# Strassen products of an expert kernel: common sums kept in PSUM, products of neighbouring steps interleaved, PReLU as a signed maximum, token sums of the attention on GpSimd

## The chip, the cores and the metric

The kernel runs on one core of one Trainium2 chip. The metric is the device time of one execution in microseconds (us). The engines are named as in the profile: PE is TensorE (matmul), PEld its weight loads, DVE VectorE, ACT ScalarE, POOL GpSimd, and SP SyncE, whose queue issues all DMAs here. Each of PE, DVE, ACT, POOL and SP works through its own instructions in the order in which the program gives them, and waits at the first one whose semaphores are not there yet.

## The reference

Three layers follow each other. Only what matters is shown.

```python
# 1. decayed linear attention, B=2, H=8, S=768, D=64 (tokens: B*S = 1536, width H*D = 512)
state = gamma * state + k_t v_t^T ;  y_t = scale * q_t . state
x = y.transpose(0, 2, 1, 3).reshape(1536, 512)
# 2. eight dense experts, F = 1024, gate made doubly stochastic in 8 rounds
P = exp(x @ w_gate - max); 8 times: P /= P.sum(1) + 1e-9; P /= P.sum(0) + 1e-9; P *= N / E
out = sum over e of P[:, e:e+1] * (np.maximum(x @ w1[e], 0) @ w2[e])
# 3. one layer of width 2048 with a learned slope per hidden unit
h = out @ w_in
y = (np.maximum(h, 0) + alpha * np.minimum(h, 0)) @ w_out
```

## The kernel before

The kernel has an attention stage and then 20 phases. A phase is one half of the tokens (768) through one block of 1024 hidden units: phases 0 to 15 are the two halves through the eight experts, phases 16 to 19 the two halves through the two halves of layer 3 (called the PReLU phases here, since their hidden units are max(h, 0) + alpha min(h, 0)). All products are fp32 split into a high and a low part, three matmuls for each (`mm3`).

A phase has two parts. In the first (L1 here), x times w1 is made by a Strassen-Winograd scheme for each of four column blocks j (n counts these steps over all phases): seven products of 6 matmuls each, `product(ph, j, p)`, in the order p = 1, 5, 6, 7, 4, 2, 3. Product 1 opens a PSUM bank, and product 2 is added into it; product 5 opens one, and product 3 is added into it; 6, 7 and 4 each have their own. `after` makes the four output blocks out of them: ACT copies product 1 to SBUF (`pu`, L475), DVE adds product 6 to it (L477), product 7 to that (L480), and three more additions (L481, L484, L489) make the blocks. `block` then applies Relu or PReLU and leaves a high part `hh` and a low part `hl`. The low part is put off by one product (`late`). In a PReLU phase a block is ACT Relu of -h (L458), ACT times -alpha (L459), DVE max and add (L460), ACT high part (L461), DVE low part (L462). In the second part (L2 here), `layer2` multiplies the blocks by w2, six tiles t0 to t5 of 48 matmuls of 512 columns.

The order of everything else is a table of hooks (`at`), each run behind one product or one tile: the splits of the next weights (`w1_adds`, `w1_part`, `w2_split`, with an ACT copy for the high part and POOL or DVE for the low part), the gate's rounds (`shift`, `cols`), decoding of the float64 weights of layer 3 (`decode`), the transposed copies of the experts' output for layer 3 (`turn`, in phases 8 and 16), and the sums of x that the scheme needs (`x_sums`, seven pieces for each of two k).

The attention stage runs 12 steps of 128 tokens: `prep(i+1)` (k scaled on POOL, L235), `scores` (PE, then DVE times the mask into A, L224), `state` (PE, then DVE scales the state into T, L261), `outs` (PE, then DVE, L297), `gate`. The dictionary `early` puts the weight splits and the x sums of phase 0 (L139 to L149, on DVE) behind steps 2 to 11.

## Time and profile before

| what | value |
|---|---|
| median of 3 runs | 1444.62 us (1437.99 to 1685.13) |
| profiled execution, time | 1439.99 us |
| its span, first to last instruction | 1438.2 us |
| mean granted TensorE clock | 0.969 |
| PE / DVE / ACT / POOL busy | 94% / 58% / 38% / 36% of the span |

The profiled execution has 1.8 us around its span and lies 4.6 us under the median of the three runs. Busy time of PE is counted from pipelined matmuls, so 94% doesn't say that PE has no time to give; the stages have to be looked at apart.

### The profile page before, as it was taken

Reading aid. Unit: us, or ns where it says so; the run is one execution under the profiler, and the core shown is the slowest. Engines: PE = TensorE matmul, PEld = TensorE weight load, DVE = VectorE, ACT = ScalarE, POOL = GpSimd, SP = SyncE. Lnnn points to the kernel's source line nnn. Section 1 sums busy time; section 2 is a strip of 40 time slices with the busy share of each in tenths; the row PEclk is TensorE's granted clock in tenths of the full one; section 3 lists DMA queues with packets and bytes.
Section 4 is the critical chain, followed back from the end, with each engine's and each line's share of the span. In section 5 each row is a group of like instructions: output and inputs, shape, how many; then the busy total and the mean of one; then the engine's idle time right before and its main releaser. Section 6 shows DMA issues by size and latency. Waiting matters only on the chain.

```text
span 1438.2 us, 18384 instructions
## 1 busy us (share of the span) xinstructions
PE 1356.9 (94%) x7045; PEld 1208.8 (84%) x7046; DVE 833.6 (58%) x1526; ACT 543.5 (38%) x979; POOL 520.7 (36%) x393
## 2 busy tenths in 40 slices
PE   9789999999999999999999999999998797887978
PEld 7688989889898988989898898989897677676876
DVE  4856565766666665766666666645457424564351
ACT  0242514243241423534242433414235626455360
POOL 3551515245251524426151543615243305042140
PEclk9899999999999999999999999999999898998989
DMA  8531223343342334244333333213032312221001
GB/s 300 179 104 53 87 84 107 97 119 92 110 125 81 110 96 124 83 124 118 101 110 96 103 98 108 84 56 89 30 125 63 101 35 74 80 81 59 30 30 44
DMA packets 45448, 136.25 MB, mean 95 GB/s; under 512 B 5169, under 2 KB 10289, under 8 KB 45361
## 3 DMA queue, kind: packets, MB, share of 16 engines
q1 hardware_dynamic: 45360, 135.08, 30.3%
q8 instruction: 55, 0.90, 0.2%
...
## 4 chain that ended last, share of the span: by engine, by line
PE 68%; issue 10%; ACT 7%; DVE 7%; POOL 6%; DMA 2%; SPq 0%; POOLq 0%; DVEq 0%; ACTq 0%
PE o L124 15%; PE o L122 15%; PE o L123 15%; PE p L124 7%; PE p L122 7%; PE p L123 7%; ACT n L459 3%; DVE p L460 2%; ACT n L458 2%; ACT hh L461 1%; DMA xd<-tt 1%; DMA kv<-in_kv_dram 1%; DVE p L481 1%; DVE u L480 1%; PE sc L216 1%
## 5 line engine op out<-in xcount | busy, mean ns | idle before, releaser
L92 POOL TENSOR_TENSOR s<-raw 128x256 f32<-128x256 f32 x42 | 37.5, 892 | 506.3 <-DVE wc69l L83 31.8
L451 ACT ACTIVATE hh<-p 128x384 fp32r<-128x384 f32 x256 | 120.4, 490 | 162.7 <-DVE p L481 135.1
L452 DVE SCALAR_TENSOR_TENSOR hl<-p,hh 128x384 fp32r<-128x384 f32 x256 | 136.5, 554 | 58.2 <-ACT hh L451 48.7
L520 DVE SCALAR_TENSOR_TENSOR acc<-o,P,acc 128x512 f32<-128x512 f32 x84 | 62.9, 749 | 153.2 <-PE o L124 153.2
L477 DVE TENSOR_TENSOR pu<-p,pu 128x384 f32<-128x384 f32 x80 | 44.5, 556 | 94.1 <-PE p L124 86.0
L411 ACT ACTIVATE ex<-ex,ebias 128x512 uint32<-128x512 uint32 x32 | 23.2, 725 | 193.3 <-DVE ex L410 188.5
L460 DVE SCALAR_TENSOR_TENSOR p<-p,n 128x384 f32<-128x384 f32 x64 | 36.3, 567 | 91.4 <-ACT n L459 91.4
L475 ACT ACTIVATE pu<-p 128x384 f32<-128x384 f32 x80 | 39.2, 490 | 65.1 <-PE p L124 65.0
L480 DVE TENSOR_TENSOR u<-p,pu 128x384 f32<-128x384 f32 x80 | 44.6, 557 | 21.5 <-PE p L124 17.5
L489 DVE TENSOR_TENSOR p<-p,pu 128x384 f32<-128x384 f32 x80 | 44.9, 562 | 14.4 <-PE p L124 13.8
L481 DVE TENSOR_TENSOR p<-p,u 128x384 f32<-128x384 f32 x80 | 45.3, 567 | 2.8
L461 ACT ACTIVATE hh<-p 128x384 fp32r<-128x384 f32 x64 | 31.5, 492 | 40.5 <-DVE p L460 40.5
L484 DVE TENSOR_TENSOR p<-p,u 128x384 f32<-128x384 f32 x80 | 44.5, 556 | 0.0
L458 ACT ACTIVATE n<-p 128x384 f32<-128x384 f32 x64 | 31.3, 490 | 31.3 <-DVE p L481 22.4
L410 DVE TENSOR_SCALAR ex<-rd 128x512 uint32<-128x512 uint32 x32 | 19.5, 609 | 39.5 <-DMA rd<-in_w_out_dram 19.9
L459 ACT ACTIVATE n<-n,nal 128x384 f32<-128x384 f32 x64 | 39.4, 616 | 2.1
L514 ACT ACTIVATE acc<-o 128x512 f32<-128x512 f32 x18 | 10.8, 598 | 75.3 <-PE o L124 75.3
L95 POOL TENSOR_TENSOR raw<-raw,s 128x256 f32<-128x256 f32 x42 | 35.4, 843 | 3.3
L462 DVE TENSOR_TENSOR hl<-p,hh 128x384 fp32r<-128x384 f32 x64 | 35.2, 550 | 1.6
L94 POOL TENSOR_TENSOR s<-raw 128x256 f32<-128x256 f32 x42 | 34.2, 814 | 0.0
L93 POOL TENSOR_TENSOR s<-s,raw 128x256 f32<-128x256 f32 x42 | 31.8, 758 | 3.3
L148 ACT ACTIVATE xh<-ta 128x384 fp32r<-128x384 f32 x16 | 8.4, 526 | 62.2 <-DVE ta L139 60.4
...
## 6 DMA issues: line engine op xcount, KB each, us to landing
raw<-in_w_dram SPq DMA_DIRECT2D x128, 512.0 KB, 3.7
raw<-wd SPq DMA_DIRECT2D x32, 512.0 KB, 3.3
rd<-in_w_in_dram SPq DMA_DIRECT2D x16, 512.0 KB, 4.2
...
rd<-in_w_out_dram SPq DMA_DIRECT2D x16, 512.0 KB, 4.2
qk<-in_qkT_dram SPq DMA_DIRECT2D x12, 512.0 KB, 5.1
kv<-in_kv_dram SPq DMA_DIRECT2D x12, 512.0 KB, 5.6
...
```

The costliest lines, as they stand in the source:

```text
L122: nc.tensor.matmul(ps, ah, bh, start=first, stop=False, skip_group_check=True)
L123: nc.tensor.matmul(ps, ah, bl, start=False, stop=False, skip_group_check=True)
L124: nc.tensor.matmul(ps, alo, bh, start=False, stop=last, skip_group_check=True)
L451: nc.scalar.activation(out=hi, in_=src, func=AF.Relu)
L452: late.append(lambda: nc.vector.scalar_tensor_tensor(out=lo, in0=src, scalar=0.0, in1=hi.bitcast(F32), op0=ALU.max, op1=ALU.subtract))
L458: nc.scalar.activation(out=neg, in_=src, func=AF.Relu, scale=-1.0)
L459: nc.scalar.activation(out=neg, in_=neg, func=AF.Copy, scale=nal[:, f:f + 1])
L460: nc.vector.scalar_tensor_tensor(out=src, in0=src, scalar=0.0, in1=neg, op0=ALU.max, op1=ALU.add)
L461: nc.scalar.activation(out=hi, in_=src, func=AF.Copy)
L480: nc.vector.tensor_tensor(out=u, in0=ps, in1=pu[n][:, 1], op=add)
L481: nc.vector.tensor_tensor(out=ps, in0=banks[n, 5], in1=u, op=add)
L520: nc.vector.scalar_tensor_tensor(out=acc[t], in0=ps, scalar=p, in1=acc[t], op0=ALU.mult, op1=ALU.add)
```

## The change

What it does, part by part:

- The sums that several blocks share are kept in PSUM. ACT copies product 1 from its bank A into a second bank B, and product 6 is added into B by PE. Product 5 is copied to SBUF (`d`, by ACT in expert phases, by DVE in PReLU phases). DVE writes B + d into a bank E, into which product 3 is added; product 7 is added into B; DVE writes B + d over bank D as the (1,1) block; product 4 is added into B as the (1,0) block. Four banks are written once by a matmul of ones before their first use (`seeded`).
- The products of step j stand between those of step j-1: (j,1), (j,5), (j-1,4), (j,6), (j-1,3), (j,2), (j,7).
- PReLU is max(s h, s alpha h) times s with s = -1 where alpha > 1 and 1 elsewhere: ACT makes s alpha h, and one product later DVE the maximum and ACT the high part, and one later DVE the low part.
- The x sums of phase 0 go to POOL in pieces, behind steps 6 to 11; the splits of step 0's weights come earlier, those of step 1's weights go to DVE behind the attention; k is scaled on ACT from step 7 on (eight instructions for each). s and s alpha are made on DVE at the start.
- Hooks of the weight splits move; `turn` uses plain fp32 matmuls with the identity in place of transposes; the gate's column sums go to other columns of a bank that DVE clears first.

```diff
@@ start of the attention stage
-            nc.scalar.activation(out=nal, in_=al, func=AF.Copy, scale=-1.0)
+            nc.vector.tensor_scalar(out=sg, in0=al, scalar1=1.0, scalar2=-2.0, op0=ALU.is_gt, op1=ALU.mult)
+            nc.vector.tensor_scalar_add(sg, sg, 1.0)
+            nc.vector.tensor_tensor(out=sa, in0=sg, in1=al, op=ALU.mult)
@@ prep
+                    if i <= NCH:
...
+                    else:
+                        for h in range(H):
+                            nc.scalar.activation(
+                                out=k_t[i][:, h, :], in_=kv_t[i][:, 0, h, :], func=AF.Copy, scale=Gk[:, c, h:h + 1]
+                            )
@@ early
+            xs = [x_pieces(0, k, xf[:, k, :], xf[:, 2 + k, :], pool) for k in range(2)]
             early = {
...
+                1: [lambda: w_load(0, 0)],
+                2: [lambda: w1_adds(0, pool)],
+                3: [lambda: w1_part(0, "a", pool), lambda: w_load(0, 1)],
+                4: [lambda: w1_part(0, "c", pool), lambda: w_load(1, 0)],
+                5: [lambda: w1_part(0, "b", pool), lambda: w_load(1, 1)],
+                6: xs[0][0:2],
+                7: xs[0][2:5],
+                8: xs[0][5:7],
+                9: xs[1][0:2],
+                10: xs[1][2:5],
+                11: xs[1][5:7],
@@ behind the attention
             nc.vector.tensor_copy(P, gt)
+            w1_adds(1, nc.vector)
+            for part in "acb":
+                w1_part(1, part, nc.vector)
@@ product
+        def seeded(name):
+            ps = bank(name)
+            if made[0] < 4:
+                made[0] += 1
+                nc.tensor.matmul(ps, one[:, 0:128], one, start=True, stop=True)
+            return ps[:, 0:HT]
...
-            key = {2: 1, 3: 5}.get(p, p)
+            key = {1: "A", 2: "A", 5: "D", 6: "B", 7: "B", 4: "B", 3: "E"}[p]
@@ block, PReLU
-            nc.scalar.activation(out=neg, in_=src, func=AF.Relu, scale=-1.0)
-            nc.scalar.activation(out=neg, in_=neg, func=AF.Copy, scale=nal[:, f:f + 1])
-            nc.vector.scalar_tensor_tensor(out=src, in0=src, scalar=0.0, in1=neg, op0=ALU.max, op1=ALU.add)
-            nc.scalar.activation(out=hi, in_=src, func=AF.Copy)
-            late.append(lambda: nc.vector.tensor_tensor(out=lo, in0=src, in1=hi.bitcast(F32), op=ALU.subtract))
+            nc.scalar.activation(out=t, in_=src, func=AF.Copy, scale=sa[:, f:f + 1])
+            def largest():
+                nc.vector.scalar_tensor_tensor(out=src, in0=src, scalar=s1, in1=t, op0=ALU.mult, op1=ALU.max)
+                nc.scalar.activation(out=hi, in_=src, func=AF.Copy, scale=s1)
+            late.append([largest, lambda: nc.vector.scalar_tensor_tensor(
+                out=lo, in0=src, scalar=s1, in1=hi.bitcast(F32), op0=ALU.mult, op1=ALU.subtract
+            )])
@@ after
+            if p == 5:
+                d = banks[n, "d"] = tmp.tile([128, HT], F32, tag="d", bufs=2, name=f"d{n}")
+                if PHASES[ph][1] < E:
+                    nc.scalar.activation(out=d, in_=banks[n, "D"], func=AF.Copy)
+                else:
+                    nc.vector.tensor_copy(d, banks[n, "D"])
+            elif p == 1:
+                banks[n, "B"] = seeded(f"B{n}")
+                nc.scalar.activation(out=banks[n, "B"], in_=banks[n, "A"], func=AF.Copy)
             elif p == 6:
-                nc.vector.tensor_tensor(out=pu[n][:, 1], in0=ps, in1=pu[n][:, 0], op=add)
+                banks[n, "E"] = seeded(f"E{n}")
+                nc.vector.tensor_tensor(out=banks[n, "E"], in0=banks[n, "B"], in1=banks[n, "d"], op=add)
             elif p == 7:
...
+                nc.vector.tensor_tensor(out=banks[n, "D"], in0=banks[n, "B"], in1=banks[n, "d"], op=add)
@@ turn
-                nc.tensor.transpose(ps[:, 128 * q:128 * q + 128], acc[3 * h + q][:, 128 * a:128 * a + 128], ident)
+                nc.tensor.matmul(
+                    ps[:, 128 * q:128 * q + 128], acc[3 * h + q][:, 128 * a:128 * a + 128], ident,
...
@@ hooks and order
-                at(ph, (j, 4), lambda m=m: w1_part(m, "c", pool))
-                at(ph, (j, 3), lambda m=m: w1_part(m, "a", pool))
-                at(ph, (j + 1, 5), lambda m=m: w1_part(m, "b", pool))
-            for j, key in enumerate(((0, 2), (1, 2), (2, 6), (3, 6))):
+                at(ph, (j, 2), lambda m=m: w1_part(m, "a", pool))
+                at(ph, (j, 7), lambda m=m: w1_part(m, "c", pool))
+                at(ph, (j, 3), lambda m=m: w1_part(m, "b", pool))
+            for j, key in enumerate(((2, 1), (2, 2), (3, 1), (2, 3))):
...
-        order = [(j, p) for j in range(NJ) for p in (1, 5, 6, 7, 4, 2, 3)] + [f"t{t}" for t in range(TT)]
+        order = [(0, 1), (0, 5), (0, 6), (0, 2), (0, 7)]
+        for j in range(1, NJ):
+            order += [(j, 1), (j, 5), (j - 1, 4), (j, 6), (j - 1, 3), (j, 2), (j, 7)]
+        order += [(NJ - 1, 3), (NJ - 1, 4)] + [f"t{t}" for t in range(TT)]
```

How the instructions stand, at three places. First ACT in one round (one j) of a PReLU phase, phase 17, before: `pu` is product 1, `n` the scaled block, `hh` the high part of a block, and `w` and `v` are splits of weights.

```order
L475 ACTIVATE pu_10908<-p_1_10901 128x384
L82 ACTIVATE wb70h<-raw_70_10667 128x512
L458 ACTIVATE n_11_10949<-p_7_10937 128x384
L459 ACTIVATE n_11_10949<-n_11_10949,nal 128x384
L461 ACTIVATE hh_11_10947<-p_7_10937 128x384
L458 ACTIVATE n_10_10964<-p_4_10954 128x384
L459 ACTIVATE n_10_10964<-n_10_10964,nal 128x384
L461 ACTIVATE hh_10_10962<-p_4_10954 128x384
L82 ACTIVATE wc71h<-s_10911 128x768
```

The same engine in a round of the same phase now; A, B, D and E are the PSUM banks.

```order
L532 ACTIVATE B_10719<-A_10712 128x384
L502 ACTIVATE hh_11_10701<-D_10631,sg 128x384
L83 ACTIVATE v68h<-raw_68_10233 128x1024
L498 ACTIVATE n_10_10748<-B_10621,sa 128x384
L502 ACTIVATE hh_10_10746<-B_10621,sg 128x384
L498 ACTIVATE n_01_10768<-E_10657,sa 128x384
L83 ACTIVATE wb71h<-raw_71_10496 128x512
L498 ACTIVATE n_00_10785<-A_10712,sa 128x384
L502 ACTIVATE hh_01_10766<-E_10657,sg 128x384
L83 ACTIVATE v69h<-raw_69_10287 128x1024
L498 ACTIVATE n_11_10804<-D_10730,sa 128x384
L502 ACTIVATE hh_00_10783<-A_10712,sg 128x384
```

A block has two ACT instructions in place of three, and between them stands the first one of the next block; in this round two `v` splits stand between them as well.

Second, DVE at the start of the program, before (A is the masked scores of step 0, `al` the slopes):

```order
L208 MEMSET ones 128x128
L224 TENSOR_TENSOR A_178<-sc_0_179,mask 128x4x128
L224 TENSOR_TENSOR A_178<-sc_1_180,mask 128x4x128
L261 TENSOR_TENSOR T_122<-st_196,tab 64x4x64 x2
L224 TENSOR_TENSOR A_216<-sc_0_217,mask 128x4x128
```

And now:

```order
L218 TENSOR_SCALAR sg<-al 128x16
L219 TENSOR_SCALAR sg<-sg 128x16
L220 TENSOR_TENSOR sa<-sg,al 128x16
L225 MEMSET ones 128x128
L241 TENSOR_TENSOR A_185<-sc_0_186,mask 128x4x128
L241 TENSOR_TENSOR A_185<-sc_1_187,mask 128x4x128
```

Three instructions on the slopes stand ahead of the first masked scores; the DMA of the slopes keeps its place on SP.

Third, DVE behind step 6 of the attention, before (`xc` is the step's output, `xl` the low parts of the x pieces, T the scaled state):

```order
L297 TENSOR_TENSOR xc_518<-y_509,tab 128x512
L139 TENSOR_TENSOR ta_0_529<-xf 128x384
L140 TENSOR_TENSOR ta_0_529<-xf,ta_0_529 128x384
L141 TENSOR_TENSOR tb_0_530<-xf 128x384
L142 TENSOR_TENSOR tb_0_530<-xf,ta_0_529 128x384
L149 TENSOR_TENSOR xl_0_163<-xf,xh_0_162 128x384
...
L149 TENSOR_TENSOR xl_0_167<-xf,xh_0_166 128x384
L261 TENSOR_TENSOR T_121<-st_483,tab 64x4x64 x2
L224 TENSOR_TENSOR A_561<-sc_0_562,mask 128x4x128
```

And now:

```order
L321 TENSOR_TENSOR xc_542<-y_533,tab 128x512
L285 TENSOR_TENSOR T_122<-st_500,tab 64x4x64 x2
L241 TENSOR_TENSOR A_577<-sc_0_578,mask 128x4x128
L241 TENSOR_TENSOR A_577<-sc_1_579,mask 128x4x128
L321 TENSOR_TENSOR xc_603<-y_590,tab 128x512
```

The eleven instructions of the x sums are gone from between `xc` and T.

## Rows read from the trace of the kernel before

**Rows 1.** The page: busy us, share of the span and instructions of each engine.

```profile
PE 1356.9 (94%) x7045; PEld 1208.8 (84%) x7046; DVE 833.6 (58%) x1526; ACT 543.5 (38%) x979; POOL 520.7 (36%) x393
```

**Rows 2.** Busy time by stretch; columns in the first line, PEclk is the granted clock.

```profile
core 0: us, PE busy (x) PEld busy (x) DVE busy (x) ACT busy (x) POOL busy (x), PEclk, DMA share, GB/s
0.00:76.10 76.10, 64.76 (x739) 54.16 (x740) 48.75 (x81) 11.88 (x22) 31.48 (x37) 0.91 0.67 231
76.10:114.60 38.50, 34.13 (x175) 33.21 (x176) 25.41 (x58) 16.01 (x30) 20.97 (x14) 0.91 0.33 101
148.70:1093.60 944.90, 938.35 (x4707) 844.40 (x4706) 587.56 (x1043) 345.32 (x615) 370.79 (x270) 1.00 0.33 98
1031.40:1061.10 29.70, 29.52 (x170) 29.20 (x169) 18.28 (x34) 15.97 (x29) 20.97 (x14) 1.00 0.28 91
1061.10:1093.60 32.50, 32.50 (x145) 26.88 (x144) 22.08 (x41) 10.74 (x21) 3.76 (x4) 1.00 0.30 95
1093.60:1434.50 340.90, 285.51 (x1273) 249.06 (x1272) 152.54 (x290) 163.30 (x301) 94.23 (x68) 0.90 0.18 58
1184.10:1229.40 45.30, 35.48 (x170) 34.04 (x169) 22.22 (x43) 29.23 (x53) 20.94 (x14) 0.85 0.18 59
45.90:52.70 6.80, 3.35 (x33) 3.04 (x34) 6.16 (x10) 0.00 (x0) 3.48 (x3) 0.50 0.05 16
```

**Rows 3.** Timeline of phase 17: one PReLU block on ACT and DVE, idle in brackets.

```profile
1203.03 0.49 ACT L458 ACTIVATE n<-p 128x384 f32<-128x384 f32 x1 [1.37 <-DVE p L481]
1203.55 0.61 ACT L459 ACTIVATE n<-n,nal 128x384 f32<-128x384 f32 x1
1204.20 0.57 DVE L460 SCALAR_TENSOR_TENSOR p<-p,n 128x384 f32<-128x384 f32 x1 [1.21 <-ACT n L459]
1204.80 0.49 ACT L461 ACTIVATE hh<-p 128x384 fp32r<-128x384 f32 x1 [0.63 <-DVE p L460]
1205.27 0.50 ACT L458 ACTIVATE n<-p 128x384 f32<-128x384 f32 x1
```

**Rows 4.** The page's DMA issues: the weights' loads, KB, median us to landing.

```profile
raw<-in_w_dram SPq DMA_DIRECT2D x128, 512.0 KB, 3.7
```

**Rows 5.** Timeline of the attention stage: start, duration, instruction, idle before it.

```profile
8.61 1.29 DVE L224 TENSOR_TENSOR A<-sc,mask 128x512 f32<-128x512 f32 x2 [7.62 <-DMA mask<-in_cmask_dram]
...
11.58 1.09 PE L284 MATMUL y<-A,kv 128*64 128x128 f32 x16
...
14.27 1.16 PE L274 MATMUL y<-qk,T 128*128 128x128 f32 x8
...
14.61 0.21 ACT L203 ACTIVATE nal<-al 128x16 f32<-128x16 f32 x1 [12.59 <-DMA al<-in_alpha_dram]
...
17.37 0.69 PE L250 MATMUL st<-kv,k 128*64 128x64 f32 x16
...
22.18 0.69 PE L250 MATMUL st<-kv,k 128*64 128x64 f32 x16
...
44.79 3.69 DVE L149 TENSOR_TENSOR xl<-xf,xh 128x384 fp32r<-128x384 f32 x2
...
49.35 1.12 PE L250 MATMUL st<-kv,k 128*64 128x64 f32 x16 [4.77 <-issue]
...
64.60 1.12 PE L250 MATMUL st<-kv,k 128*64 128x64 f32 x16 [4.06 <-issue]
```

**Rows 6.** Timeline of phase 8: three transposes and the matmul behind them.

```profile
596.01 0.49 PE L535 MATMUL tr<-ident,acc 128*128 128x128 f32 x3
596.25 0.42 PE L122 MATMUL p<-xh,wb32h 128*128 128x384 f32 x1
```

**Rows 7.** Groups of the attention stage: count, busy us, mean ns of one, idle.

```profile
L83 POOL TENSOR_TENSOR wa0l<-raw,wa0h 128x512 fp32r<-128x512 f32 x1 | 1.3, 1273 | 0.0
L82 ACT ACTIVATE wc1h<-s 128x768 fp32r<-128x768 f32 x1 | 0.8, 843 | 3.0 <-POOL s L94 3.0
```

**Rows 8.** Timeline of the attention stage: two ACT copies behind each other.

```profile
42.98 0.92 ACT L148 ACTIVATE xh<-xf 128x384 fp32r<-128x384 f32 x2
```

More of the change, by code (lines that the diff above doesn't have):

```diff
@@ L359, in shift @@
         def shift():
-            ps = bank("mx")
-            nc.tensor.matmul(ps[:, 0:128], ones, sums["m"], start=True, stop=True)
+            ps = bank("mx")[:, HT:512]
+            nc.vector.memset(ps, 0.0)
+            nc.tensor.matmul(ps, ones, sums["m"], start=False, stop=True, skip_group_check=True)
             nm = sp.tile([128, 1], F32, tag="nm", name="nm")
-            nc.vector.tensor_reduce(out=nm, in_=ps[:, 0:128], axis=AX.X, op=ALU.max)
+            nc.vector.tensor_reduce(out=nm, in_=ps, axis=AX.X, op=ALU.max)
             nc.vector.tensor_scalar_mul(nm, nm, -1.0)
@@ L380, in cols @@
         def cols(it):
-            ps = bank(f"cs{it}")
-            nc.tensor.matmul(ps[:, 0:E], ones, sums[it], start=True, stop=True)
+            ps = bank(f"cs{it}")[:, HT:HT + E]
+            nc.vector.memset(ps, 0.0)
+            nc.tensor.matmul(ps, ones, sums[it], start=False, stop=True, skip_group_check=True)
             g = sp.tile([128, E], F32, tag="g", name=f"g{it}")
-            nc.vector.tensor_scalar_add(g, ps[:, 0:E], 1e-9)
+            nc.vector.tensor_scalar_add(g, ps, 1e-9)
             nc.vector.reciprocal(out=g, in_=g)
@@ L426, in decode @@
                 decode_load(then)
-        banks, pu, hq, late = {}, {}, {}, []
+        banks, hq, late = {}, {}, []
+        made = [0]
+        def seeded(name):
[4 more added lines that the diff above has]
+            return ps[:, 0:HT]
         def product(ph, j, p):
             n = NJ * ph + j
-            key = {2: 1, 3: 5}.get(p, p)
-            if key == p:
-                banks[n, p] = bank(f"p{n}_{p}")[:, 0:HT]
+            key = {1: "A", 2: "A", 5: "D", 6: "B", 7: "B", 4: "B", 3: "E"}[p]
+            if p in (1, 5):
+                banks[n, key] = bank(f"{key}{n}")[:, 0:HT]
             ps = banks[n, key]
@@ L441, in product @@
                 ks = slice(128 * k, 128 * k + 128)
-                mm3(ps, wh[:, ks], wl[:, ks], xh[:, k, :], xl[:, k, :], k == 0 and key == p, k == 1)
+                mm3(ps, wh[:, ks], wl[:, ks], xh[:, k, :], xl[:, k, :], k == 0 and p in (1, 5), k == 1)
             after(ph, n, j, p)
@@ new lines, in largest, with step_late @@
+            def largest():
[3 more added lines that the diff above has]
+                out=lo, in0=src, scalar=s1, in1=hi.bitcast(F32), op0=ALU.mult, op1=ALU.subtract
+            )])
+        def step_late(steps):
+            for fns in steps:
+                fns.pop(0)()
+                if fns:
+                    late.append(fns)
@@ L464, in flush @@
         def flush():
             while late:
-                late.pop(0)()
+                steps = list(late)
+                late.clear()
+                step_late(steps)
         def after(ph, n, j, p):
             add = ALU.add
-            ps = banks[n, {2: 1, 3: 5}.get(p, p)]
             before = list(late)
             late.clear()
-            if p == 1:
-                pu[n] = tmp.tile([128, 2, HT], F32, tag="pu", bufs=2, name=f"pu{n}")
-                nc.scalar.activation(out=pu[n][:, 0], in_=ps, func=AF.Copy)
+            if p == 5:
[7 more added lines that the diff above has]
+                nc.scalar.activation(out=banks[n, "B"], in_=banks[n, "A"], func=AF.Copy)
@@ L482, in after @@
-                block(ph, n, j, 1, 1, ps)
+                nc.vector.tensor_tensor(out=banks[n, "D"], in0=banks[n, "B"], in1=banks[n, "d"], op=add)
+                block(ph, n, j, 1, 1, banks[n, "D"])
             elif p == 4:
-                nc.vector.tensor_tensor(out=ps, in0=ps, in1=pu[n, 3], op=add)
-                block(ph, n, j, 1, 0, ps)
+                block(ph, n, j, 1, 0, banks[n, "B"])
             elif p == 2:
-                block(ph, n, j, 0, 0, ps)
+                block(ph, n, j, 0, 0, banks[n, "A"])
@@ L488, in after @@
             elif p == 3:
-                nc.vector.tensor_tensor(out=ps, in0=ps, in1=pu[n][:, 1], op=add)
-                block(ph, n, j, 0, 1, ps)
-            for fn in before:
-                fn()
+                block(ph, n, j, 0, 1, banks[n, "E"])
+            step_late(before)
         acc, ob = {}, {}
@@ L534, in turn @@
             for q in range(3):
-                nc.tensor.transpose(ps[:, 128 * q:128 * q + 128], acc[3 * h + q][:, 128 * a:128 * a + 128], ident)
+                nc.tensor.matmul(
+                    ps[:, 128 * q:128 * q + 128], acc[3 * h + q][:, 128 * a:128 * a + 128], ident,
+                    start=(q == 0), stop=(q == 2), skip_group_check=True,
+                )
             t = tp.tile([128, HT], F32, tag="tmp", name=f"tt{g}_{a}{h}")
```

68 lines of the change are left out of this document (33 added, 35 removed).

## The prediction, made before the changed kernel ran

> **What bounds the kernel now.** I read the page first: PE is busy for 94% of the span, every other engine for 58% or less [rows 1]. That is a mean over stages, so next comes busy time by stretch. Phase 15 (1031.4 to 1093.6) shows what a phase costs when nothing holds PE: L1 29.7 us, nearly all of it PE, with the weight loads busy for 29.2 of them, and L2 32.5 us, at full clock [rows 2]. 168 matmuls in 29.7 us are 0.177 us each, 1.06 us a product. No part of the change takes matmuls away, so 62.2 us a phase is the floor that I measure the rest against. Phases 1 to 15 take 944.9 us [rows 2]; 15 floors are 933.0, and the 24 transposes of phase 8 add 8 x 0.24 = 1.9 (three of them push the next matmul back by 0.24 us [rows 6]). So at most 10 us lie there, although DVE is busy for 587.6 us of that stretch [rows 2].
>
> The four PReLU phases are another matter: 340.9 us against 4 x 62.2 + 1.9 = 250.7, so 90.2 us are lost, with the clock at 0.90 of full speed [rows 2]. In L1 of phase 17 (45.3 us) PE is busy for 35.5, ACT for 29.2, DVE for 22.2: nobody is full. The timeline says why. ACT starts a block at 1203.03, waits 0.63 us inside it for DVE's result, and starts the next block at 1205.27 [rows 3]: 2.24 us of ACT's queue per block, four blocks, 9 us for a round whose seven products need 7.4; the copy of product 1 and the weight splits come on top. The queue of ACT with its wait inside each block is the bound there, and PE stops, and its clock falls to half, behind it.
>
> The attention stage with phase 0's L1 takes 76.1 + 38.5 us [rows 2]. A step lasts 4.81 us (17.37 to 22.18) and PE has no gap in it, but two gaps of 4.77 and 4.06 us stand before `state` [rows 5]. In front of the first, DVE is at the x sums until 48.48 (two low parts in 3.69 us), and its T, which `state` waits for, comes behind them. After each gap the clock is at 0.50 for 6.8 us [rows 2]; I put that at 1.5 to 2.3 us each, since `state`, 0.69 us otherwise, takes 1.12 [rows 5] and the next instructions are stretched alike.
>
> **The change, part by part.** *Expert phases.* Per round DVE loses three of its five additions and ACT gains a copy. Three times 0.57 (the DVE time of such a block [rows 3]) in 64 rounds is 109 us of DVE work, but PE has only those 10 us to win; I take 8 and let 2 stand for new waits. The new handoffs: product 1, copy A to B, product 6; product 6, E, product 7; product 7, D, product 4. In a round from j = 1 on, two products, 2.1 us, stand between each pair; the engine needs 0.5 to 0.6. In round 0 and at the end of L1 one product stands between, 1.06 us, still more. A transfer queue is touched too: the w2 splits stand later, in rounds 2 and 3, and the load of the third part waits until POOL has read the first. POOL has about 15 us of w1 work ahead of it in L1, its low part of 1024 columns is about 2 x 1.27 = 2.5 us [rows 7], which ends near 19, and the load takes 3.7 [rows 4], so it lands 23 to 24 us into L1 where ACT asks for it at 22. ACT then stands 1 to 2 us, with Relu parts and one copy `d` queued behind; the additions behind these still have a product of slack. L2 needs that part only 2.7 us after its start. I cost this at nothing; if the slack is gone it is up to 1 us a phase.
>
> *PReLU phases.* A block now has two ACT instructions, and between them stands the next block's first one, so ACT no longer waits inside a block. Both are scaled by a column: 0.61 us each, as the scaled copy now [rows 3]. In L1 that is 4 x (8 x 0.61 + 0.49) = 21.5 us, and the splits (six of w1, four of w2; by columns from 768 in 0.84 [rows 7]) 8.5: 30.0 us by durations against PE's 29.7. But copies behind each other overlap: two of 0.51 take 0.92 [rows 8], so 10% comes off, 27 us. DVE has eleven instructions a round, 11 x 0.57 = 6.3 of 7.4 us. Both fit, ACT closely: in round 2, with two w2 splits and one of w1, it has 7.3 us of work in 7.4. Late ACT delays the copy to B first, which has 1.5 us of slack. L2 hides the rest: the last block's high part is wanted only at the 22nd matmul of t0, 4.7 us in. So I let 1.5 us a phase stand. In phase 16 the transposed copies need the same two buffers as the scaled blocks and hold them until their stores land, and the stores now queue on SP behind weight loads that wait for POOL: 3 us more. Gain: 90.2 - 4 x 1.5 - 3 = 81.2. The bounds are 90 (no wait) and 65 (5 us a phase, 5 in phase 16).
>
> *Transposes as plain matmuls.* This costs. The attention's fp32 matmul of the same shape is two instructions, four take 1.16 us [rows 5], about 0.28 each, against 0.08 for a transpose. 48 x 0.2 = 9.4 us, on PE's own path, where nothing hides it.
>
> *Attention.* The gaps go, since T has no x sums ahead of it on DVE: 8.8 us and 3.8 of slow clock, 12.6. But DVE's first instruction now waits for the slopes, whose DMA lands at 14.6 (ACT's wait for it [rows 5]). The first mask product stood at 8.61, and 1.3 us later y could start; now three short instructions and a memset, some 0.8 us together, end at about 15.4, A at 16.7, and y starts at 16.8 where it was 11.58 [rows 5]: 5.2 us, and 1.5 of slow clock behind it, so 6.7 lost. Step 0 has no other work for PE in that time.
>
> POOL's 22 instructions on x start when six steps are done, some 42 us in now. By columns from 512 in 1.27 us [rows 7] one is about 1.0; eight waits for an ACT copy between a sum and its low part are 0.6 each; 26.8 us, and ACT's k scaling puts them some 4 later, at about 73. PE is done with the attention at 76.1 - 12.6 + 6.7 = 70.2 and takes product 1 and 5 to 72.3. Then it needs the copy to B, which is queued on ACT behind the last x copy (72) and three splits of step 1's weights (0.6, 0.84, 0.6): 74.7. So PE waits 2.4 us, and I give 1 to the clock. Phase 0's L1 has 38.5 - 29.7 = 8.8 of excess now, of which 1.5 are small matmuls that stay (four seeds among the new ones); from 7.3 it falls to 3.4, since `shift` and `cols`, in front of the additions on DVE today, now have two products of slack behind E. Gain: 3.9. Together 12.6 - 6.7 + 3.9 = 9.8, between 0 and 15.
>
> The rule of the Trainium skill against this part is GPSIMD Engine Reference, section 4.1 Engine selection: elementwise work on two inputs belongs on VectorE, GpSimd being about twice as slow. By that ratio to DVE's 0.57 us for a block of this size [rows 3], an estimate from that section, one of the 22 takes 1.14 us, the chain ends 3 us later and the time is 1353. Whichever of the two prices holds, the trace speaks for the move: on DVE the x sums cost PE 12.6 us, and on POOL they end some 3 us after the attention. No row shows POOL at this work.
>
> **Sum.** 8 + 81.2 + 9.8 - 9.4 = 89.6. The profiled execution's span, 1438.2, becomes 1348.6, and with the 1.8 us around it **1350 us**; that is 90 us under the profiled execution's 1440.0, and 94 under the median of 1444.6, which I take as the scatter of three runs.
>
> **The rivals.** *ACT stays the bound of the PReLU phases.* For it: 30.0 us by durations, and a wait for DVE's maximum in front of each high part. If copies don't overlap and the 0.63 us stays in all 16 blocks, ACT needs 40 us an L1, 9 more than I gave, 36 in four phases, with 10 of slow clock: 1396. Against it: between the two ACT instructions DVE has a whole product's time.
>
> *POOL's x sums hold up phase 0.* If one takes 1.3 instead of 1.0 us (two engines at SBUF at once, as in the 3.69 us of two low parts on DVE), the chain ends 6.6 us later, ACT's queue with it, and the wait at product 6 is 9 us: 1357, and about 1360 with a gap before a `state`, since k is scaled on ACT behind the same copies.
>
> *Slower than before.* The mechanism is the handoffs through one bank: product, ACT or DVE, product, three in each of 80 rounds. Today PE seldom waits for these engines in expert phases. If ACT's and DVE's queues run later than their slack in each, PE stops 240 times. The gain of 90 is gone at 0.37 us each, a 2% loss is reached at 0.5, and at 0.6 the time is 1494. Against it: the slack of 1.5 us, and ACT at 16 of 29.7 us in an expert L1 [rows 2].
>
> *Less work than it seems.* If the sums in PSUM were the point, the DVE time saved should count; by the floor it doesn't, and the forecast already has the expert phases at 8.
>
> **Chances.** Forecast 0.66 (1332 to 1355); x sums late 0.14 (1355 to 1365); ACT bound in part or whole 0.12 (1365 to 1400); better than 1332 0.06, were all of PReLU's 90, MoE's 10 and 15 of the attention won (1334 by the sum); slower 0.02. The range 1332 to 1385 leaves out the better end and the worst of the ACT case. About 2% is what a measurement of this kernel can tell from no change. All cases but one are more than 2% under the time before; for what I haven't seen I leave 0.04 for no change and 0.02 for slower, so faster 0.94.
>
> **What would show it.** Right: L1 of phases 17 to 19 at 30 to 32 us and L2 at 32.5, clock 1.00 there; phases 1 to 15 at 62 to 63; phases 8 and 16 some 5 us longer for plain matmuls; DVE's first instruction at 14.6 and a PE gap of 5 us before the first y; no gap before `state` later; one wait of some 2 us at product 6 of phase 0. Wrong: waits of PE for the bank B or D in every round, an ACT above 95% in PReLU L1s, or expert phases above 64 us.

## The result, and the profile after

The changed kernel takes **1390.0 us** (median of 4 runs, 1388.6 to 1391.8), against 1444.2 for the kernel before on the same chip: ratio 0.964, interval 0.961 to 0.9665. It is faster by 3.6%, as forecast in sign, but 40 us later than the 1350 and outside the range. The 1444.2 is the median of four runs of which one took 1685.1, in a slower state of the chip, and the ratio leaves that run out. The profiled span is 1387.3 us.

The page of the changed kernel, busy time of each engine (as [rows 1]): PE does the same products with fewer gaps, DVE has lost 123 us.

```profile
PE 1340.4 (97%) x7098; PEld 1199.7 (86%) x7098; DVE 710.5 (51%) x1299; ACT 544.7 (39%) x1010; POOL 536.0 (39%) x404
```

Busy time by stretch of the changed kernel (as [rows 2]): attention, phase 0's L1 and its L2, phases 1 to 15, L1 of phase 8, phase 15's L1 and L2, the PReLU phases, and L1 of phases 16, 17 and 18.

```profile
core 0: us, PE busy (x) PEld busy (x) DVE busy (x) ACT busy (x) POOL busy (x), PEclk, DMA share, GB/s
0.00:73.70 73.70, 64.90 (x740) 54.16 (x740) 33.63 (x62) 17.25 (x49) 34.33 (x42) 0.93 0.70 238
73.70:111.30 37.60, 33.52 (x178) 31.20 (x179) 23.21 (x58) 20.49 (x38) 26.74 (x21) 0.95 0.32 90
111.30:161.60 50.30, 40.13 (x159) 31.54 (x157) 18.93 (x62) 7.01 (x12) 3.28 (x5) 0.90 0.12 42
161.60:1112.80 951.20, 941.79 (x4732) 850.66 (x4731) 489.54 (x858) 369.24 (x670) 375.02 (x270) 1.00 0.32 98
601.30:643.10 41.80, 37.73 (x217) 37.41 (x216) 17.22 (x33) 23.83 (x46) 21.76 (x15) 0.92 0.32 97
1050.90:1080.10 29.20, 29.20 (x170) 29.16 (x169) 11.87 (x23) 17.50 (x33) 19.64 (x14) 1.00 0.28 90
1080.10:1112.80 32.70, 32.70 (x146) 27.06 (x146) 19.60 (x37) 8.62 (x17) 5.08 (x5) 1.00 0.29 97
1112.80:1383.50 270.70, 260.06 (x1297) 232.15 (x1295) 144.54 (x262) 130.75 (x241) 96.60 (x69) 0.99 0.23 73
1112.80:1156.50 43.70, 37.33 (x218) 35.93 (x216) 25.98 (x47) 27.24 (x52) 21.94 (x15) 0.96 0.30 93
1189.40:1219.10 29.70, 29.64 (x170) 29.05 (x169) 19.37 (x35) 21.28 (x39) 18.90 (x14) 1.00 0.27 86
1252.20:1287.60 35.40, 31.44 (x170) 30.54 (x169) 24.41 (x44) 22.75 (x42) 19.43 (x14) 0.95 0.26 87
```

Set beside my sum, stage by stage, in us of span:

| stage | before | forecast | after | later than forecast |
|---|---|---|---|---|
| attention | 76.1 | 70.2 | 73.7 | 3.5 |
| phase 0, L1 | 38.5 | 34.6 | 37.6 | 3.0 |
| phase 0, L2 | 34.1 | 34.1 | 50.3 | 16.2 |
| phases 1 to 15 | 944.9 | 941.6 | 951.2 | 9.6 |
| phases 16 to 19 | 340.9 | 264.4 | 270.7 | 6.3 |

The 16.2 stand in a stage of which I had said nothing. Of the 9.6 in phases 1 to 15, 5.0 are phase 8 (its L1 goes from 32.1 to 41.8 us, of which 4.7 were forecast) and the rest the other phases, which won 3.5 us and not 8. (A tile of L2 is 24 matmuls, so that six make 144, and not 48 as the section on the kernel before has it; the row of phase 15's L2 counts 146.) What PE waits for most in the changed kernel, in us in total, times, and the longest:

```profile
PE B L123 <- ACT B L532: 16.4, 12, 4.1
PE cs L413 <- DVE cs L412: 12.7, 6, 3.1
PE y L308 <- DVE A L241: 5.3, 1, 5.3
PE D L123 <- ACT tt L593: 1.9, 1, 1.9
...
PE mx L391 <- DVE mx L390: 1.4, 1, 1.4
```

The second and the last are the gate (`cols` and `shift`): seven waits, 14.1 us. The timeline of the changed kernel in phase 0's L2 shows one such wait:

```profile
125.03 0.60 ACT L567 ACTIVATE acc<-o 128x512 f32<-128x512 f32 x1 [6.88 <-PE o L125]
125.52 0.83 ACT L83 ACTIVATE wc4h<-s 128x768 fp32r<-128x768 f32 x1
126.25 0.62 ACT L83 ACTIVATE wb4h<-raw 128x512 fp32r<-128x512 f32 x1
126.39 0.96 DVE L84 TENSOR_TENSOR wc4l<-s,wc4h 128x768 fp32r<-128x768 f32 x1 [4.82 <-ACT wc4h L83]
127.26 0.68 DVE L84 TENSOR_TENSOR wb4l<-raw,wb4h 128x512 fp32r<-128x512 f32 x1
127.95 0.07 DVE L412 MEMSET cs<- 128x8 f32 x1
...
128.07 0.39 PE L413 MATMUL cs<-s,ones 128*128 128x8 f32 x2 [3.08 <-DVE cs L412]
```

The clear of the bank takes 0.07 us, but it stands in DVE's queue behind two low parts of weight splits, these wait for ACT's high parts, and those for an ACT copy of the output tile that PE has just finished. PE, which needs the bank for its next instruction, stops for 3.08 us, and its clock falls behind it (the granted clock is 0.90 over the whole L2).

The first is the copy of product 1 to B; 12 of its 16.4 us stand at the start of phases 8, 16 and 18. The timeline of the changed kernel at the start of phase 8:

```profile
606.09 0.55 DVE L145 TENSOR_TENSOR tb<-b,ta 128x384 f32<-128x384 f32 x1
606.68 0.52 ACT L147 ACTIVATE xh<-tb 128x384 fp32r<-128x384 f32 x1 [1.15 <-DVE tb L145]
607.11 0.47 ACT L532 ACTIVATE B<-A 128x384 f32<-128x384 f32 x1
...
607.63 0.69 PE L123 MATMUL B<-xh,wc32h 128*128 128x384 f32 x1 [4.07 <-ACT B L532]
```

`x_pieces` makes sum, high part and low part of one piece before the next sum, so ACT waits 1.15 us for DVE in front of the high parts that need a sum, and the copy to B is queued behind them all.

### The profile page after: what moved, and what is told of

Same layout as the page of the kernel before. It is cut to its first block, busy times and chain, and to the rows that moved or that the text cites. A ratio compares the mean times of both kernels' runs of the same rounds, so it can differ in the third digit from the quotient of the medians.

```text
span 1387.3 us, 18259 instructions
## 1 busy us (share of the span) xinstructions
PE 1340.4 (97%) x7098; PEld 1199.7 (86%) x7098; DVE 710.5 (51%) x1299; ACT 544.7 (39%) x1010; POOL 536.0 (39%) x404
## 5 line engine op out<-in xcount | busy, mean ns | idle before, releaser
L93 POOL TENSOR_TENSOR s<-raw 128x256 f32<-128x256 f32 x41 | 37.8, 923 | 464.7 <-DVE wc5l L84 36.4
L535 DVE TENSOR_TENSOR E<-B,d 128x384 f32<-128x384 f32 x80 | 45.2, 565 | 139.7 <-PE B L125 118.8
L537 DVE TENSOR_TENSOR D<-B,d 128x384 f32<-128x384 f32 x80 | 45.3, 567 | 88.9 <-PE B L125 88.9
L490 ACT ACTIVATE hh<-E 128x384 fp32r<-128x384 f32 x64 | 31.5, 493 | 56.5 <-PE E L125 56.5
L532 ACT ACTIVATE B<-A 128x384 f32<-128x384 f32 x80 | 38.7, 483 | 37.7 <-PE A L125 37.7
L491 DVE SCALAR_TENSOR_TENSOR hl<-E,hh 128x384 fp32r<-128x384 f32 x64 | 35.5, 555 | 23.8 <-ACT hh L490 23.8
L490 ACT ACTIVATE hh<-D 128x384 fp32r<-128x384 f32 x64 | 31.3, 490 | 29.2 <-DVE D L537 29.2
L491 DVE SCALAR_TENSOR_TENSOR hl<-A,hh 128x384 fp32r<-128x384 f32 x64 | 35.2, 550 | 11.2 <-ACT hh L490 11.2
L491 DVE SCALAR_TENSOR_TENSOR hl<-D,hh 128x384 fp32r<-128x384 f32 x64 | 35.6, 556 | 5.8 <-ACT hh L490 0.8
L491 DVE SCALAR_TENSOR_TENSOR hl<-B,hh 128x384 fp32r<-128x384 f32 x64 | 35.1, 549 | 1.3 <-ACT hh L490 1.2
L490 ACT ACTIVATE hh<-B 128x384 fp32r<-128x384 f32 x64 | 31.4, 491 | 10.7 <-PE B L125 10.3
L94 POOL TENSOR_TENSOR s<-s,raw 128x256 f32<-128x256 f32 x41 | 31.8, 775 | 3.2
```

Of the source, the lines that this page charges most:

```text
L93: eng.tensor_tensor(out=s[:, 0], in0=a21, in1=a22, op=ALU.add)
L94: eng.tensor_tensor(out=s[:, 1], in0=s[:, 0], in1=a11, op=ALU.subtract)
L490: nc.scalar.activation(out=hi, in_=src, func=AF.Relu)
L491: late.append([lambda: nc.vector.scalar_tensor_tensor(out=lo, in0=src, scalar=0.0, in1=hi.bitcast(F32), op0=ALU.max, op1=ALU.subtract)])
L532: nc.scalar.activation(out=banks[n, "B"], in_=banks[n, "A"], func=AF.Copy)
L535: nc.vector.tensor_tensor(out=banks[n, "E"], in0=banks[n, "B"], in1=banks[n, "d"], op=add)
```

## The experiments

Each ratio is to runs of the kernel before on the same chip (median 1441 to 1442 us); "after" is the changed kernel. Times of a whole kernel are medians; times of a stage and waits come from its one profiled execution, and a stage that an edit doesn't touch can differ by 3 us between two of them: the attention ends at 73.6 to 77.1 in after, e2 and e4, and phase 16's L1 takes 43.7 to 47.3 in after, e1 and e3.

**e1: the clears of the gate's bank on PE.**

```diff
-            ps = bank(f"cs{it}")[:, HT:HT + E]
-            nc.vector.memset(ps, 0.0)
+            full = bank(f"cs{it}")
+            nc.tensor.matmul(full, zeros, one, start=True, stop=True)
+            ps = full[:, HT:HT + E]
```

and the same for `mx`. 

> The changed kernel (1390.0 us, span 1387.3) with one edit: the bank of each of the gate's nine matmuls of ones is cleared by a bf16 matmul of zeros on PE and not by a DVE memset. Theory 1: PE waits for the memset, which stands on DVE behind the low parts of weight splits (eight gaps before `cs` and `mx` of 1.2 to 3.1 us, 15 us, and half clock behind them). Then phase 0's L2 falls from 50.2 to 34 to 36 us, its L1 from 37.6 to 33 to 35, and the time to about 1372. Rival: the row and column sums themselves come late on DVE; the gaps stay, now released by `s`, L2 stays at 45 to 50, the time at 1385 to 1392.

Measured: 1372.4 us, ratio 0.951 (0.950 to 0.953). Phase 0's L1 takes 35.4 us, its L2 35.6 at full clock (columns as in the stretches above):

```profile
75.50:110.90 35.40, 33.54 (x180) 31.65 (x183) 23.59 (x55) 20.12 (x38) 25.21 (x20) 0.95 0.31 95
110.90:146.50 35.60, 35.47 (x162) 28.39 (x162) 18.05 (x56) 7.23 (x13) 4.23 (x5) 1.00 0.19 60
```

No wait before `cs` or `mx` is left. A clear by matmul takes 0.39 us on PE; the nine clears by DVE cost 17.6 us, in seven waits of 14.1 us and the slower clock behind them. Shown.

**e2: the x sums for phases 8, 16 and 18 in the order of before** (four sums, then seven times high and low part; their slices are left out).

```diff
-        for run in x_pieces(g, k, b1, b2, nc.vector):
-            run()
+        nc.vector.tensor_tensor(out=ta[:, 0], in0=b12, in1=b11, op=ALU.subtract)
...
+        nc.vector.tensor_tensor(out=tb[:, 1], in0=b21, in1=ta[:, 1], op=ALU.subtract)
...
+        for q, src in order:
+            hi, lo = (t[:, k, :] for t in X[g][q])
+            nc.scalar.activation(out=hi, in_=src, func=AF.Copy)
+            nc.vector.tensor_tensor(out=lo, in0=src, in1=hi.bitcast(F32), op=ALU.subtract)
```

> The changed kernel with one edit: on DVE (the sums for phases 8, 16 and 18) the four sums stand first again and the seven copies and low parts behind them. Theory 1: the copy of product 1 to bank B waits on ACT behind x copies that each wait for their own sum; with the sums first ACT is through them some 3 us sooner, the gap of 3.9 to 4.1 us at product 6 falls under 1.5, L1 of phases 8, 16 and 18 falls by 4 to 6 us each with the clock, and the time is 1373 to 1378. Rival: DVE needs the same time for the eleven instructions in either order and the copies end as late; the gap stays, the time is 1387 to 1391.

Measured: 1372.3 us, ratio 0.952 (0.950 to 0.953). L1 of phase 8 falls from 41.8 to 34.7, of phase 16 from 43.7 to 37.9, of phase 18 from 35.4 to 29.7: 18.6 us in three places, and the three long waits for the copy to B are gone.

```profile
602.40:637.10 34.70, 34.70 (x217) 34.69 (x216) 14.36 (x29) 21.53 (x42) 21.14 (x14) 1.00 0.44 116
1106.30:1144.20 37.90, 35.69 (x218) 34.62 (x217) 23.13 (x43) 24.78 (x48) 21.25 (x14) 1.00 0.34 107
1240.00:1269.70 29.70, 29.63 (x169) 29.01 (x168) 21.73 (x40) 20.48 (x37) 18.91 (x13) 1.00 0.28 95
```

Shown.

**e3: the three slope instructions behind the attention.**

```diff
@@ start of the attention stage
-            nc.vector.tensor_scalar(out=sg, in0=al, scalar1=1.0, scalar2=-2.0, op0=ALU.is_gt, op1=ALU.mult)
-            nc.vector.tensor_scalar_add(sg, sg, 1.0)
-            nc.vector.tensor_tensor(out=sa, in0=sg, in1=al, op=ALU.mult)
@@ behind the attention: the same three lines
```

> The changed kernel with one edit: the three DVE instructions on the slopes stand behind the attention. Theory 1: DVE's first instruction waits for the slopes' DMA, the first y starts 5.3 us late and the clock is at half for 6.8 us; phase 0 then starts at 66 to 67 us and not at 73.7, the time is about 1383. Rival: the later steps are held by loads of q, k and v (gaps of 0.6 and 1.4 us already now) and by the x sums on POOL, so that phase 0 starts no earlier than 70 or its product 6 waits longer; the time is 1386 to 1390.

Measured: 1384.2 us, ratio 0.9605 (0.959 to 0.962). The attention ends at 65.0 instead of 73.7, but phase 0's L1 takes 41.7 instead of 37.6: product 6 waits 3.10 us there for the copy to B (0.18 in the changed kernel). Of 8.7 us won in the attention, 5.8 stay in the median of the whole.

**e4: `turn` with transposes again.**

```diff
-                    start=(q == 0), stop=(q == 2), skip_group_check=True,
+                    is_transpose=True, start=(q == 0), stop=(q == 2), skip_group_check=True,
```

> The changed kernel with one edit: the 48 matmuls with the identity in `turn` are transposes again. Theory 1: a plain fp32 matmul of this shape is two instructions and costs PE 0.28 us against 0.08; L1 of phases 8 and 16 falls by 4 to 5 us each (41.8 to 37, 43.7 to 39), the time to about 1381. Rival: those phases are long because of waits alone (4.1 us gaps and stores that hold buffers) and the matmuls fill PE's waits: less than 1.5 us each, 1387 to 1390.

Measured: 1388.3 us, ratio 0.963 (0.9615 to 0.9645), 1.7 us less than after; the runs of the two overlap (1388.2 to 1389.8 and 1388.6 to 1391.8), so the time alone shows little. Phase 8's L1 falls by 4.2 us; phase 16's doesn't fall (44.2). That PE's wait for the copy `tt` is 2.52 us there and 1.88 in after explains nothing by itself, since e1 has 2.52 with the plain matmuls too. A cleaner pair is e2 and e7, without the long waits: phase 8's L1 falls from 34.7 to 31.8, both at full clock, and phase 16's stays (37.9 and 37.8), while PE's waits for `tt` grow from 1.76 to 3.30 us and its clock falls from 1.00 to 0.95. So 2.9 us are gained in phase 8, and in phase 16 wait and clock take the gain back.

**e5: the changed kernel with the old PReLU block.**

```diff
-            nc.scalar.activation(out=t, in_=src, func=AF.Copy, scale=sa[:, f:f + 1])
...
+            nc.scalar.activation(out=neg, in_=src, func=AF.Relu, scale=-1.0)
+            nc.scalar.activation(out=neg, in_=neg, func=AF.Copy, scale=nal[:, f:f + 1])
+            nc.vector.scalar_tensor_tensor(out=src, in0=src, scalar=0.0, in1=neg, op0=ALU.max, op1=ALU.add)
+            nc.scalar.activation(out=hi, in_=src, func=AF.Copy)
```

> The changed kernel with the PReLU block of before (Relu of -h, times -alpha, maximum and add, high part, all at once; low part late), sums in PSUM and interleaving kept. Theory 1: the new PReLU gave the PReLU phases their time back, since ACT waits inside each old block; L1 of phases 17 and 19 goes back from 29.7 to 43 to 47 us, L2 from 33 to 37 to 39, the time to 1455 to 1470. Rival: the interleaved order gives ACT the room, since a block's four instructions now have other products around them; L1 at 33 to 38, the time at 1405 to 1430.

Measured: 1451.6 us, ratio 1.007 (1.0055 to 1.009): slower than before by 0.7%, 61.6 us above after. It is a little under the theory's 1455 and far from the rival's 1405 to 1430. L1 of phases 17 and 19 takes 45.7 and 44.4, as expected, L2 34.1 us and not 37 to 39. The waits of PE in this kernel name the places:

```profile
PE B L124 <- ACT B L529: 37.9, 22, 4.1
PE B L124 <- DVE D L534: 17.1, 10, 3.1
```

With the old block the late ACT delays the copy to B, which didn't exist before. Of the 37.9 us some 16 stand in the changed kernel too, 12 of them behind the x sums of phases 8, 16 and 18; 21.9 are new, and stand in the PReLU phases, as do the 17.1 for DVE's block over D.

**e6: the kernel before with the new PReLU block alone** (the block and `late` as in the diff of the change, the three slope instructions behind the attention as in e3; all else as before). 

> The kernel before (1441.7 us) with the new PReLU alone (signed maximum, in two late steps; s and s alpha made behind the attention), old sums on DVE and old order. Theory 1: the PReLU phases fall to 62 to 65 us each as in the changed kernel, L1 at 30 to 32, the time at 1362 to 1372, and the sums in PSUM and the interleaving are not needed for it. Rival: with five additions and eight block instructions a round DVE has 7.4 us of work for PE's 7.4, and the four blocks follow each other closely; L1 stays at 34 to 38, the time at 1385 to 1405.

Measured: 1371.5 us, ratio 0.953 (0.950 to 0.956), 18.5 us less than the whole change (1.1% by the ratios). L1 of phases 17 to 19 takes 33.0, 32.9, 32.9 us, above the theory's 30 to 32 and under the rival's 34, L2 32.7 to 32.8. This one edit is worth 70 us. (Its trace is of an execution of 1379.4 us; what that is over the median stands in the attention, see e11.)

**e7: after with e1, e2, e3 and e4 together.** 

> The changed kernel with the four edits tried one by one: zeros by PE, sums of x first on DVE, slopes behind the attention, transposes. Theory 1: they cost in different places, so what they gave adds up, 17.6, 17.7, 5.8 and 1.7 us, and phase 16 gives the 4 us that the transposes couldn't while it waited: 1343 to 1350. Rival: the queues of ACT and SP at the start of phases 0 and 16 take part of it back (product 6 of phase 0 waited 3.1 us with the slopes late): 1352 to 1362.

Measured: 1343.7 us, ratio 0.932 (0.931 to 0.934). The four differences (17.6, 17.7, 5.8, 1.7) add up to 42.8, the measured one is 46.3. The 4 us that the transposes were to give in phase 16 didn't come (L1 37.8, see e4).

**e8: e2 with phase 0's x sums on DVE too**, behind steps 6 and 8 as before.

```diff
-                6: xs[0][0:2],
...
-                11: xs[1][5:7],
+                6: [lambda: x_sums(0, 0, xf[:, 0, :], xf[:, 2, :])],
+                8: [lambda: x_sums(0, 1, xf[:, 1, :], xf[:, 3, :])],
```

> The kernel of the second run (sums of x first, 1372.3 us) with the x sums of phase 0 on DVE behind steps 6 and 8, as before. Theory 1: T stands behind them again, two gaps of 4 to 5 us before `state` come back with half clock behind them, phase 0 starts at 84 to 88 us and not at 77, the time is 1379 to 1384. Rival: what the gaps cost POOL's slower sums cost too, by ACT's k scaling behind them and the late start of phase 0's product 6; the time stays at 1369 to 1375.

Measured: 1370.3 us, ratio 0.951 (0.950 to 0.953); e2 took 1372.3. That is the rival's time: the theory, with gaps of 4 to 5 us and 1379 to 1384, is refuted. With the weight splits moved, moving the sums to POOL as well won nothing. The reason is in the low parts. DVE's timeline in e8, behind step 6:

```profile
51.18 1.02 DVE L177 TENSOR_TENSOR xl<-ta,xh 128x384 fp32r<-128x384 f32 x2
...
53.05 1.02 DVE L177 TENSOR_TENSOR xl<-xf,xh 128x384 fp32r<-128x384 f32 x2
53.99 0.85 DVE L298 TENSOR_TENSOR T<-st,tab 64x256 f32<-64x256 f32 x2
```

Two low parts take 1.02 us, where two took 3.69 before [rows 5]. In the kernel before, POOL's timeline has these rows at that time; in e8 POOL is idle from 44 to 66 us.

```profile
44.71 1.81 POOL L83 TENSOR_TENSOR wc0l<-s,wc0h 128x768 fp32r<-128x768 f32 x1 [2.61 <-ACT wc0h L82]
46.49 1.57 POOL L83 TENSOR_TENSOR wb0l<-raw,wb0h 128x512 fp32r<-128x512 f32 x1
```

POOL's first instruction ends at 46.52, its second at 48.06, and DVE's two low parts end at 46.94 and 48.48, 0.42 us behind each: a DVE instruction that stands until POOL's is done. The Trainium skill, page "SBUF — State Buffer", section "SBUF: two separate sides", says just that: a DVE instruction with two inputs in SBUF and a GpSimd instruction that reads SBUF exclude each other for a whole instruction. The rows agree, also in what is not held up: T, which has one input in PSUM, takes its usual 0.85 us for two beside POOL's `k`.

```profile
48.03 1.35 POOL L235 TENSOR_TENSOR k<-kv,tab 128x512 f32<-128x512 f32 x1
48.40 0.85 DVE L261 TENSOR_TENSOR T<-st,tab 64x256 f32<-64x256 f32 x2
```

**e9: e7 with the x sums on DVE** (the edit of e8). 

> This kernel is the one of e7_all with the token sums of phase 0 back on DVE, behind steps 6 and 8 of the attention. Theory: the gaps before state in the kernel before came from POOL's weight splits running at the same time as DVE's token sums (two low parts 3.69 us there, 1.02 us in e8_x_on_dve, where POOL was idle), and not from DVE having the sums; so with the splits done earlier the sums cost DVE 6 to 7 us in each of two places without a long gap, and the time is within 3 us of 1343.7, that is 1341 to 1347. Rival: DVE's work itself holds T and state up once the first 5 us of the attention aren't lost any more; then gaps of 3 to 5 us come back before two steps, with slow clock behind them, and the time is 1351 to 1357.

Measured: **1340.0 us**, ratio 0.930 (0.928 to 0.931), the fastest of all and 1 us under the range expected. The attention ends at 66.5 (69.8 in e7) and the longest gap before `state` is 1.24 us. Once the early waits are gone, the x sums seem to cost some 3.7 us more on POOL than on DVE; the intervals just touch.

**e10: e7 with the stores of `turn` on ACT's queue.**

```diff
-            nc.sync.dma_start(out=xd[g][:, a, HT * h:HT * h + HT], in_=t)
+            nc.scalar.dma_start(out=xd[g][:, a, HT * h:HT * h + HT], in_=t)
```

> This kernel is the one of e7_all with the stores of the turned blocks issued from ACT's queue in place of SP's. Theory: in phase 16 the store waits on SP behind a weight load, the copy that needs its buffer waits 1.7 us for it on ACT, and PE stops 2.8 us; issued from ACT at once, the wait goes, phase 16's L1 falls from 37.8 to 33 to 35 us, and the time is 1339 to 1342. Rival: the store was issued within 0.5 us anyway (the load ahead of it on SP takes 0.32 us to issue) and takes some 4 us because it shares the DMA engines with the load of 512 KB; then phase 16 stays at 36 to 39 us, and the time at 1342 to 1348.

Measured: 1341.5 us, ratio 0.931 (0.929 to 0.932); phase 16's L1 35.8 instead of 37.8. The store lands in 2.7 us (median) instead of 4.0 around that place, PE's wait falls from 2.79 to 0.92. L1 lies between the two expectations, the time inside the theory's range next to its border, and the interval overlaps e7's: that the wait hangs on the store is shown, but not how much of the time is SP's queue and how much the transfer.

**e11: the kernel before with only its weight splits moved** as in the changed kernel; the x sums stay on DVE behind steps 6 and 8.

```diff
-                4: [lambda: w_load(1, 0), lambda: w1_adds(0, pool)],
...
+                2: [lambda: w1_adds(0, pool)],
+                3: [lambda: w1_part(0, "a", pool), lambda: w_load(0, 1)],
+                4: [lambda: w1_part(0, "c", pool), lambda: w_load(1, 0)],
+                5: [lambda: w1_part(0, "b", pool), lambda: w_load(1, 1)],
...
             nc.vector.tensor_copy(P, gt)
+            w1_adds(1, nc.vector)
+            for part in "acb":
+                w1_part(1, part, nc.vector)
```

> The kernel before with only its weight splits of the attention moved as in the changed kernel (step 0's behind steps 1 to 5 on POOL, step 1's behind the attention on DVE); the token sums stay on DVE behind steps 6 and 8. Theory: the two gaps of 4.77 and 4.06 us before state were DVE's token sums slowed down by POOL's splits at the same time; without the overlap the low parts take 0.5 us each, the gaps fall below 1.5 us, the attention ends at 64 to 69 instead of 76.1, phase 0's L1 may give back 1 to 3 us for the splits on DVE, and the time is 1430 to 1435. Rival: the eleven DVE instructions are too many wherever POOL is; the gaps stay at 3 us or more, the attention ends at 73 or later, and the time is 1438 to 1445.

Measured: 1435.2 us, ratio 0.9956 (0.994 to 0.997). The gaps before `state` fall from 4.77 and 4.06 to 2.11 and 1.94, the attention ends at 71.8. The time is at the edge of what the theory gave, the attention and the gaps lie between the two. What stays can be told apart by the durations of the eleven DVE instructions. One of them takes 0.55 us alone. In three kernels 22 of them take longer, each beside a POOL instruction, and each ends 0.41 to 0.42 us behind the end of one. Added up, for both places (the gap is PE's before `state`, all in us):

| kernel | two gaps | time of the longer ones beyond 0.55 each | rest |
|---|---|---|---|
| before | 8.83 | 6.46 | 2.37 |
| e6, the sums and splits as before | 13.41 | 11.03 | 2.38 |
| e11 | 4.05 | 1.71 | 2.34 |
| e9, `k` on ACT, POOL idle | 2.32 | 0.00 | 2.32 |

So nearly three quarters of the two gaps before (6.5 of 8.8 us) was POOL in DVE's way: 4.8 went with the splits, 1.7 stay in e11, since POOL's `k` still meets DVE's last sum once in each place. The rest, 2.3 to 2.4 us in all four, is what having the sums on DVE costs PE when POOL is out of the way, about a quarter of the gaps. (In all of them `state` starts 0.10 us behind T's end; the releaser that a profile names there, "issue" in before and ACT in e9, isn't what it waited for.) The two meetings in e11:

```profile
42.77 1.04 POOL L235 TENSOR_TENSOR k<-kv,tab 128x512 f32<-128x512 f32 x1 [2.79 <-DMA kv<-in_kv_dram]
42.81 1.42 DVE L142 TENSOR_TENSOR tb<-xf,ta 128x384 f32<-128x384 f32 x1
...
56.56 1.44 POOL L235 TENSOR_TENSOR k<-kv,tab 128x512 f32<-128x512 f32 x1 [5.92 <-PE st L250]
57.02 1.40 DVE L142 TENSOR_TENSOR tb<-xf,ta 128x384 f32<-128x384 f32 x1
```

## Why the prediction was right in sign and wrong in size

**The step that failed** is the term for the gate in phase 0: "`shift` and `cols`, in front of the additions on DVE today, now have two products of slack behind E". I looked at what they delay on DVE, and not at the new line in them, the clear of the bank, which makes PE wait for DVE's queue. I put the gate at a gain of 3.9 in L1 and at nothing in L2; L1 came out 0.9 shorter, L2 16.2 longer, and the clears cost 17.6 us (e1).

**A second term was missing.** The change also gives phases 8, 16 and 18 their x sums in a new order. I costed the move of the sums to POOL in phase 0, and in the expert phases only the handoffs, for which "the engine needs 0.5 to 0.6", as if its queue were empty. At the start of these phases ACT's queue holds the x copies, and the copy to B stands behind them: 17.7 us (e2). I had written that late ACT "delays the copy to B first", for PReLU phases; the same sentence held here. The two together are 35.3 of the 38.6 us by which the stages came later; the rest is a balance of smaller misses both ways.

**PReLU: right, in mechanism and size.** L1 of phases 17 and 19 takes 29.7 us (30 to 32 forecast), L2 32.8 to 33.3, the clock is 1.00 there. The timeline of the changed kernel in phase 17 shows ACT, which stood inside each block before [rows 3]:

```profile
1195.45 0.58 ACT L498 ACTIVATE n<-D,sa 128x384 f32<-128x384 f32 x1 [0.54 <-DVE D L537]
...
1195.97 0.58 ACT L502 ACTIVATE hh<-A,sg 128x384 fp32r<-128x384 f32 x1
...
1196.07 0.63 DVE L501 SCALAR_TENSOR_TENSOR D<-D,sg,n 128x384 f32<-128x384 f32 x1
...
1196.45 0.84 ACT L83 ACTIVATE wc70h<-s 128x768 fp32r<-128x768 f32 x1
...
1197.19 0.48 ACT L532 ACTIVATE B<-A 128x384 f32<-128x384 f32 x1
...
1197.60 0.56 ACT L502 ACTIVATE hh<-D,sg 128x384 fp32r<-128x384 f32 x1
```

Between the scaled block `n<-D` and its high part `hh<-D` stand another block's high part, a split and the copy to B, and the maximum (1196.07) is done meanwhile. ACT is busy for 21.3 of 29.7 us, so it fits with more room than the 27 forecast. With the x order mended the four phases take 259.2 (e2), against 264.4 forecast. Alone the edit is worth 70 us (e6), in the changed kernel 62 (e5).

**Expert phases: the floor held.** The 14 phases without 0 and 8 go from 62.87 to 62.62 us each, 3.5 us in all; I took 8 for fifteen. 123 us less DVE work bought almost nothing, as the floor said. The PSUM sums aren't idle, though: with the new PReLU an L1 of phases 17 to 19 takes 33 us without them and the interleaved steps (e6) and 29.7 with both.

**Attention: one term sized right, one reason wrong, the end 3.5 us late.** DVE's first instruction, in the changed kernel's timeline, waits for the slopes until 14.10 (14.6 forecast), and PE 5.30 us before y (5.2 forecast):

```profile
14.10 1.04 DVE L218 TENSOR_SCALAR sg<-al 128x16 f32<-128x16 f32 x1 [14.10 <-DMA al<-in_alpha_dram]
...
15.61 1.22 DVE L241 TENSOR_TENSOR A<-sc,mask 128x512 f32<-128x512 f32 x2
16.38 1.83 PE L308 MATMUL y<-A,kv 128*64 128x128 f32 x12 [5.30 <-DVE A L241]
```

It cost 8.7 us in the attention and 5.8 net (e3), for 6.7 forecast. The attention ended 3.5 us later than the sum had it; of this, waits of PE for the load of q and k (1.41 us) and for POOL's `k` (0.62) weren't forecast, and the rest isn't traced. "The gaps go, since T has no x sums ahead of it on DVE": they went, but the sums by themselves were a quarter of them and POOL in the sums' way three quarters (e11); e8, with the sums on DVE and POOL out of the way, has no long gap either. So the term held with most of its reason missing. My sentence that "on DVE the x sums cost PE 12.6 us" was a reading of two rows without POOL's rows beside them. The forecast wait of 2.4 us at product 6 was 0.18 here. One profile doesn't size it: e4 and e2, the same up to there, waited 1.47 and 0.99, e3, whose attention ended at 65.0, 3.10, and e7, whose attention ended at 69.8, near the 70.2 forecast, 0.27. What sets it is open.

**Plain matmuls: the mechanism right, the size too large.** Three blocks cost 0.35 us more as plain matmuls, 2.8 for the eight places of a phase, as in phase 8 between e2 and e7 (2.9), where 4.7 was forecast; the 4.2 of e4 lies between two stages at granted clocks of 0.92 and 0.95. In phase 16 nothing came, since PE waited for the copies `tt` anyway, and not "on PE's own path, where nothing hides it". (48 x 0.2 is 9.6, not 9.4.)

**The rivals.** The slower one, handoffs stopping PE in every round, didn't happen: PE waits 12 times for the copy to B, 16.4 us in all, most of it in three places. It is real with the old PReLU block (e5), which ends slower than before. "Less work than it seems" was the nearest: the sums themselves moved the time little. POOL's x sums took 1.00 us each, as forecast and not 1.3; they and the attention both ended 3.5 to 3.7 us later than in my sum. ACT as the bound of the PReLU phases didn't happen: their L1 takes 29.7 us where no x order is in the way.
